# Batch 0's input products in float32 from decoded, unsplit weights, and a float64 decoding by one multiplication and two merging passes, in a fused attention and gated feed-forward kernel

## The chip, the cores and the metric

One core of a Trainium2 chip runs the whole program in one launch. The metric is the device time of one execution in microseconds. Lower is better.

## The reference, cut to what matters

The inputs are q, k and v, each (8 batches, 8 heads, 576 positions, 64) in float32, and the weights of a gated feed-forward layer. Attention is the sum of a local banded one (distance under 4) and one over positions averaged by fours. Its output, (8, 576, 512), is the `x` of the second function.

```python
def _attn_ref(q, k, v):
    ...
    out_d = sm_attn(q_d, k_d, v_d)
    out_up = np.repeat(out_d, factor, axis=2)
    ...
    out_local = np.matmul(attn, v)
    return (out_up + out_local).astype(np.float32)

def _moe_ref(x, w_in, w_spatial, b_spatial, w_out):
    h = np.maximum(x @ w_in, 0.0)
    u, v = (h[..., :d_ff // 2], h[..., d_ff // 2:])
    mu = np.mean(v, axis=-1, keepdims=True)
    var = np.mean((v - mu) ** 2, axis=-1, keepdims=True)
    v_n = (v - mu) / np.sqrt(var + 1e-06)
    v_s = np.einsum('ts,bsd->btd', w_spatial, v_n) + b_spatial[None, :, None]
    gated = u * v_s
    return (gated @ w_out).astype(np.float32)
```

`w_in` (512 x 1024) and `w_out` (512 x 512) arrive as float64 and are passed on as their bit patterns; `w_spatial` (576 x 576) is float32. The chip decodes the float64 itself.

## The kernel before, in words

**Units of work.** Eight heads are four pairs, two heads on 128 partitions. `attention(n)` (L610) handles one pair of one batch, 32 in all; `gated(b)` (L827) handles one batch's feed-forward layer. The engines are PE (matmul), DVE (VectorE), ACT (ScalarE), POOL (GpSimd) and SP (which issues most DMAs).

**A pair.** SP loads q and k (L624). POOL or DVE sums groups of four positions in two steps (`sum1`, `sum2`, L631 and L634). PE computes the local scores in 64 x 64 blocks of float32 (L663), with the mask added either by two matmuls of PE (L656) or by DVE (L676). DVE takes maximum, difference, sum and inverse (L685 to L698), ACT the exponential (L704), DVE or POOL the norm (L708). PE transposes the probabilities (L716), ACT copies them out (L718), PE multiplies by the values (L796). The pooled part runs beside it: scores (L728, float32, three matmuls of 144 columns), exponential (L737), norm (L749 or L751), transposes (L764), values (L782) against `tv`, the pooled v. `tv` is one plain DMA (L579) and three accumulating DMAs, which POOL issues one after the other (L581). DVE adds both parts into `xf` (L806, L808). Then x is split: ACT writes the high half, scaled to float16 (L814), DVE the low half, the difference (L816), and ACT packs the last 64 positions (L818). The scale is that of the batch: ACT sums the absolute values of v (`vabs`, L598), and `bound` (L394) makes a power of two of them by a transpose, a maximum, a spreading matmul and five short DVE instructions (L404 to L415).

**Weights.** `piece64` (L442) decodes 128 rows of 512 float64: WV and WU are the two halves of `w_in` (four pieces each), WO is `w_out` (four). DVE masks out the exponent bits (`e1`, L453), ACT rescales them (`e2`, L458), DVE puts the sign in (`e3`, L463), makes the mantissa from the high word (`m1`, L468), adds the low one (`m2`, L472), and DVE or POOL multiplies both (`m3`, L476 or L478). The result, `mb`, has five buffers. WSP is `w_spatial`, five pieces (`piece32`, `piece_tail`). WV, WU and WSP then get a common scale each (`wabs`, L558, and `bound`) and are split into a high and a low float16 half (`split`, L426 on ACT, L429 on DVE). Every product uses three of the four combinations of halves (`PAIRS`).

**A batch's feed-forward layer.** V pieces (L844): for each of four tiles of 128 positions, 3 x 4 matmuls of 512 columns; for the last 64 positions, 8 matmuls with both halves of x packed on 128 partitions (L849). Each is evicted by ACT, normalised by DVE and POOL, and split again. U pieces (L899): four feature tiles, each in two stretches of 256 and 320 positions, 12 matmuls. S pieces (L917 to L920) multiply by `w_spatial`, DVE multiplies by U, and the result is split into float32r halves; O pieces (L955) multiply by WO.

**The order.** Nothing is issued as the loops stand in the code. Every operation is handed to a `Plan` with an engine, a duration, its buffers and a rank, and `Plan.run` (L132) lays out one order for every engine: on each it takes the lowest rank among the operations that could begin within `NEAR` ns of the first. Ranks are an offset by the kind of operation (`RANK`, `MRANK`, `WRANK`) plus the pair's number. `ON` holds a letter per pair or piece, which says where an operation that has several ways runs (P for POOL, D for DVE, A for ACT, T for a mask by PE); the last letter counts for all that follow. Each engine executes its own list in order. Where the plan expects PE to idle in the first 110 us, it puts in dummy matmuls (`warm`, L992), which compute nothing. Buffers of a tag are handed out in the order in which they were asked for; the staging tiles of `piece64` (`stg`, four) thus go to WV, WU and WO in turn.

Of the kernel before, what the change touches and what calls it, by code (L numbers as in the profile page):

```python
# [76 lines left out]
class Plan:  # L77
# [19 lines left out]
    def op(self, eng, ns, fn, r=(), w=(), hold=(), after=(), rank=0.0, lag=None, port=False, kb=0, mode="",  # L97
# [8 lines left out]
        o.eng, o.ns, o.fn, o.rank, o.lag, o.port, o.kb, o.name = eng, ns, fn, rank, lag, port, kb, name  # L106
# [25 lines left out]
    def run(self, near=150.0, stay=0.0, dma=(1500.0, 4.2, 500.0), emit=True):  # L132
# [16 lines left out]
        while left:  # L149
# [60 lines left out]
            stop = t + o.ns  # L210
# [44 lines left out]
MRANK = {"V": [[-2.464, 0.981], [12.511, 0.226], [-2.435, 0.048]],
        "U0": [[8.716, 6.0], [3.119, 6.0], [7.419, 0.756]],
        "S0": [[-31.809, 0.01], [1.553, 0.075], [8.037, 1.094]],
        "U1": [[30.903, 2.091], [4.504, 0.01], [5.941, 0.268]],
        "O0": [[23.009, 0.398], [16.009, 0.093], [8.369, 0.044]],
        "S1": [[4.955, 0.875], [37.534, 0.04], [5.267, 0.763]],  # L260
        "O1": [[26.479, 0.073], [0.158, 0.01], [-14.194, 0.078]]}
EVICT = 8.0
WRANK = {"WV": [-3.775, 1.863],
        "WU": [-0.347, 0.057],
        "WSP": [3.494, 0.477],
        "WO": [5.623, 0.082]}
# [771 lines left out]
```

## Time and profile before

| What | Value |
|---|---|
| Median of 3 runs | 603.85 us (603.24 to 605.93) |
| Span of the profiled execution, first to last instruction | 603.0 us |
| PE busy | 572.9 us, 95% |
| DVE busy | 421.2 us, 70% |
| ACT busy | 352.8 us, 59% |
| POOL busy | 155.0 us, 26% |
| Moved by DMA | 56.95 MB |

The profiled execution has no time of its own beside its span; the timed runs include what lies around the span. Busy shares are means over stages with different limits, so the windows by stage are to be read beside them. Dummy matmuls count as busy. Matmuls overlap in the pipeline: a mean duration per matmul is longer than the distance of two of them, and the distance is what a piece of work costs.

### The profile page before, as it was taken

The page shows a single profiled execution, that of the slowest core. Times are in us where ns is not written, and L with a number is a line of the kernel's source. Part 1 is how long each engine was busy: PE and PEld are TensorE (multiplying, and loading weights), DVE is VectorE, ACT ScalarE, POOL GpSimd, SP SyncE. Part 2 cuts the span into 40 slices and gives each one's busy share as a digit, 9 for nine tenths or more (in the row PEclk, how much of TensorE's full clock was granted, in tenths as well). Part 3 has the DMA queues.
Part 4 walks back from the last instruction along what each step waited for, and adds up shares of the span by engine and source line. Part 5 has one row for each costly group of instructions (what it writes and reads, how often), then busy time and mean ns, then how long its engine had stood idle before and what let it go on. Part 6 is the DMA issues. An engine that isn't in the chain of part 4 may idle for free.

```text
span 603.0 us, 14807 instructions
## 1 busy us (share of the span) xinstructions
PE 572.9 (95%) x6004; PEld 421.6 (70%) x6004; DVE 421.2 (70%) x1013; ACT 352.8 (59%) x911; POOL 155.0 (26%) x165
## 2 busy tenths in 40 slices
PE   5488799999999999999999999999999999999996
PEld 2264657777688766777687858787687867775774
DVE  5499989998896865856788837875688677336230
ACT  3499779757766655665566636664566555334331
POOL 4214534204531140412322122213322122102100
PEclk9567789999999999999999999999999999999999
DMA  8886631624331641405241342305231200000002
GB/s 269 226 274 204 152 105 50 133 63 137 83 115 41 195 82 37 123 2 138 57 141 63 97 98 98 123 8 140 66 124 41 76 19 37 0 37 0 36 1 87
DMA packets 37263, 56.95 MB, mean 94 GB/s; under 512 B 3530, under 2 KB 24010, under 8 KB 37196
## 3 DMA queue, kind: packets, MB, share of 16 engines
q1 hardware_dynamic: 34892, 48.94, 25.4%
q0 software_dynamic: 2304, 7.08, 7.3%
q8 instruction: 47, 0.77, 0.5%
q14 instruction: 20, 0.16, 0.1%
HBM read 46.57 MB, written 9.44 MB: 93 GB/s over the span
## 4 chain that ended last, share of the span: by engine, by line
PE 85%; DMA 6%; ACT 4%; DVE 2%; issue 1%; POOL 1%; SPq 1%; ACTq 0%; POOLq 0%
PE pmb L917 5%; PE pma L844 5%; PE pmb L955 5%; PE pma L899 4%; PE pma L955 4%; DMA tva<-v_dram 4%; PE pmd L844 4%; PE pmc L917 4%; PE pmd L899 4%; PE pmd L955 4%; PE pmc L955 4%; PE pmb L899 4%; PE pmc L844 3%; PE pmc L899 3%; PE pma L917 3%; PE pab L796 2%
## 5 line engine op out<-in xcount | busy, mean ns | idle before, releaser
L899 PEld LDWEIGHTS <-win 128*128 128x128 f16 x768 | 74.4, 98 | 18.9 <-issue 0.9
L917 PEld LDWEIGHTS <-vha 128*128 128x128 f16 x768 | 73.4, 98 | 19.3 <-issue 0.8
L917 PE MATMUL pmb<-wsp,vha 128*128 128x320 f16 (+1 forms) x276 | 37.8, 286 | 0.0
L751 POOL TENSOR_TENSOR eda<-eda,smda 96x432 f32<-96x432 f32 x13 | 12.8, 984 | 76.7 <-ACT ua L902 37.9
L708 POOL TENSOR_TENSOR sa<-sa,sma 128x640 f32<-128x640 f32 x12 | 16.2, 1350 | 55.4 <-ACT gta L927 23.9
L917 PE MATMUL pmc<-wsp,vha 128*128 128x256 f16 (+1 forms) x216 | 28.8, 283 | 0.0
L708 POOL TENSOR_TENSOR sb<-sb,smb 128x640 f32<-128x640 f32 x14 | 19.6, 1401 | 35.6 <-PE pab L663 10.6
L872 POOL TENSOR_TENSOR stc<-stc,mhalf 128x1 f32<-128x1 f32 (+1 forms) x13 | 10.9, 838 | 53.3 <-DVE stc L856 53.3
L751 POOL TENSOR_TENSOR edb<-edb,smdb 96x432 f32<-96x432 f32 x13 | 14.4, 1105 | 39.8 <-DVE smdb L742 38.6
L917 PE MATMUL pma<-wsp,vha 128*128 128x320 f16 (+1 forms) x168 | 23.6, 290 | 0.0
L992 PE MATMUL pma<-mask_b,mask_a 128*128 128x512 bf16 x53 | 19.1, 495 | 3.2 <-DVE sw L506 3.2
L955 PE MATMUL pma<-wo,gb 128*128 128x512 f32 x84 | 21.3, 402 | 0.0
L581 POOL DMA_DIRECT2D tva<-v_dram x12 | 11.1, 927 | 31.3 <-DMA tva<-v_dram 31.2
L872 POOL TENSOR_TENSOR sta<-sta,mhalf 128x1 f32<-128x1 f32 (+1 forms) x14 | 11.4, 813 | 29.0 <-DVE sta L856 28.9
L955 PEld LDWEIGHTS pma<-wo,gb 128*128 128x128 f32 x84 | 15.6, 188 | 3.7
L955 PE MATMUL pmb<-wo,ga 128*128 128x512 f32 x72 | 18.1, 400 | 0.0
L844 PEld LDWEIGHTS <-xa 128*128 128x128 f16 x96 | 9.4, 99 | 10.9 <-issue 0.2
L638 ACT ACTIVATE qda<-kda 64x144 f32<-64x144 f32 x32 | 10.3, 321 | 11.2 <-POOL kda L634 7.4
L704 ACT ACTIVATE sb<-sb 128x640 f32<-128x640 f32 x16 | 11.8, 738 | 8.3 <-DVE sb L682 7.6
L872 POOL TENSOR_TENSOR stb<-stb,mhalf 128x1 f32<-128x1 f32 (+1 forms) x13 | 10.4, 800 | 21.4 <-DVE stb L856 21.4
L694 DVE TENSOR_REDUCE smb<-sb 128x10 f32<-128x640 f32 x16 | 12.9, 806 | 4.3 <-ACT sb L704 4.3
L955 PEld LDWEIGHTS pmb<-wo,ga 128*128 128x128 f32 x72 | 13.4, 188 | 3.2
(740 smaller groups left out, 1688.9 us busy)
## 6 DMA issues: line engine op xcount, KB each, us to landing
qka<-qk_dram SPq DMA_DIRECT2D x16, 576.0 KB, 3.7
qkb<-qk_dram SPq DMA_DIRECT2D x16, 576.0 KB, 13.6
tva<-v_dram POOLq DMA_DIRECT2D x12, 288.0 KB, 4.8
tvb<-v_dram POOLq DMA_DIRECT2D x12, 288.0 KB, 4.4
stg<-w_in_dram SPq DMA_DIRECT2D x4, 512.0 KB, 4.6
more<-w_in_dram SPq DMA_DIRECT2D x4, 512.0 KB
out_dram<-rowc SPq DMA_DIRECT2D x8, 256.0 KB, 2.1
out_dram<-rowb SPq DMA_DIRECT2D x8, 256.0 KB, 2.0
```

The costliest lines, as they stand in the source:

```text
L581: plan.op("POOL", 850, lambda r=r: nc.gpsimd.dma_start(t.ap, v4[b, r], accum_op=ALU.add), w=[t], rank=rank + 2.0 + 0.3 * r, kb=288, name="tv")
L694: nc.vector.tensor_reduce(sm.ap, s.ap, axis=AX.X, op=ALU.add)
L704: exp_of.append(plan.op("ACT", 643, lambda: nc.scalar.activation(s.ap, s.ap, AF.Exp, scale=1.0 / 8.0), w=[s], rank=R["E"], name="exp"))
L708: plan.op(nm, 0, lambda: side(nm).tensor_tensor(s.ap, s.ap, sm.ap[:, :, None].broadcast_to([P, NW, 64]), op=ALU.mult), r=[sm], w=[s], rank ...
L751: side(nd).tensor_tensor(ed.ap, ed.ap, smd.ap[:96, :, None].broadcast_to([96, 3, G]), op=ALU.mult)
L796: nc.tensor.matmul(pv.ap[h * 64:h * 64 + 64, c:c + QB[w + 1] - QB[w]], vb.ap[k, w], pT.ap[k, blk, q0:q0 + QB[w + 1] - QB[w]], start=True, ...
L844: nc.tensor.matmul(ps.ap, xs[c].ap[:, i, t * P:(t + 1) * P], win[:, c, j, FF:], start=(c == 0 and (i, j) == (0, 0)), stop=(c == NC - 1 and ...
L872: plan.op("POOL", 530, lambda: nc.gpsimd.tensor_tensor(st.ap[:r, 8:9], st.ap[:r, 8:9], mhalf[:r], op=ALU.pow), w=[st], rank=rank - EVICT, ...
L899: nc.tensor.matmul(ps.ap[:, :n], win[:, c, i, ft * P:(ft + 1) * P], xs[c].ap[:, j, HA[h]:HA[h + 1]], start=(c == 0 and (i, j) == (0, 0)), ...
L917: nc.tensor.matmul(ps.ap[:, :n], vh.ap[:, c, i, fs], wsp[:, c, j, hs], start=(c == 0 and (i, j) == (0, 0)), stop=False)
L955: nc.tensor.matmul(ps.ap, g.ap[:, c, i, k:k + P] if t < NT else gt.ap[:, c, i], wo[:, c, j, :], start=(c == 0 and (i, j) == (0, 0)), stop= ...
L992: nc.tensor.matmul(ap.rearrange("p (j k) -> p j k", k=64), mask_a, mask_b[:, None, :].broadcast_to([P, 8, 64]), start=True, stop=True)
```

## The change

It does these things:
- `piece64` decodes by four operations where it had six: `low` shifts the low word right by 29 (DVE), `shrink` multiplies the high word, read as a float32, by 2^-112 (ACT or DVE by a letter of `ON`), `body` shifts that left by three and merges the low bits (DVE), `sign` merges the sign (DVE). POOL has no part in it.
- With `FULL = 1`, batch 0 is `whole`: its x is kept in float32 in the place of its two float16 halves. `vabs`, the batch's scale, `xhi`, `xlo` and `xtail` are gone for it. Its V pieces are 4 float32 matmuls of 512 columns (five pieces, the last one not packed), its U pieces 4 float32 matmuls; both read the decoded weights `plain`, ahead of scale and split. WV and WU are still scaled and split for the batches that follow.
- The mask by PE is four matmuls on quarters of the array where it was two on the whole array; the letters of `mask` change.
- Staging tiles: three for four. `mb`: eight for five. The bias row is loaded into a tile of `xf`.
- The planner: durations are set anew, PE's work counts 1.5 times before 70 us, an accumulating DMA lands later the more is in flight, and all ranks and letters are new, so that the order of every engine differs over the whole span.

The diff, cut to its core:

```diff
+            ns = o.ns * SLOW[1] if o.mode and t < SLOW[0] else o.ns
+            stop = t + ns
...
+                more = min(4000.0, 0.5 * max(0.0, moved - t))
                 moved = max(moved, t + dma[0]) + o.kb * dma[1]
-                stop = t + dma[0] + 2 * o.kb * dma[1] + 2 * dma[2] if o.eng == "POOL" else moved + dma[2]
+                stop = t + dma[0] + 2 * o.kb * dma[1] + 2 * dma[2] + more if o.eng == "POOL" else moved + dma[2]
...
-RANK = {"load": [-0.34, 10.998, -8.45],
+RANK = {"load": [-44.57, 114.48, 16.68],
+        "vload": [85.3, -193.17, -137.58],
+        "vabs": [-38.15, -134.56, -81.97],
+        "tv": [-162.84, -70.55, 81.87],
...
-NEAR = 101.242
-STAY = 9.309
+WRANK = {"WV": [73.85, 2.37],
+        "WU": [-22.18, 0.03],
+        "WSP": [47.61, 0.01],
+        "WO": [-1.45, 9.22]}
+NEAR = 94
+STAY = 95.4
 WARM = 110000.0
-ON = {"sum": "PDPPPPDPD",
-        "m3": "PDDPPPDPDDPD",
-        "mask": "TTTTTDTTD",
-        "norm": "DDDDDPDPP",
-        "normd": "PADAAPAAP",
-        "vlo": "DPDPPPPDPPD"}
+SLOW = (70000.0, 1.5)
+FULL = 1
+MB = 8
+ON = {"shrink": "DDADAAADDA",
+      "sum": "PPDPPDDPDDDPDPDPDPPDPDPDDDPDDDPD",
+      "mask": "DDTTTDTTDTDDDDDDTDDDDDDTDDTD",
+      "norm": "DPPPDDPDPDDPPPPPPPDPDPPPDDPDPPDP",
+      "normd": "DDAAPDPDADAPDDPPPPADPPADPDDPAAD",
+      "vlo": "PDPPDPPPPDDDPDDDPPDDDPDDDDPDDDPPDPDPPPD"}
...
-    more = const.tile([P, 2, 2 * FF], F32, name="more")
-    plan.tag("stg", [stg[:, 0], stg[:, 1], more[:, 0], more[:, 1]])
+    more = const.tile([P, 2 * FF], F32, name="more")
+    plan.tag("stg", [stg[:, 0], stg[:, 1], more])
...
-    places("mb", 5, [P, FF], F32)
+    places("mb", MB, [P, FF], F32)
     places("wst", NT + 1, [P, S], F32)
-    places("bias", 1, [P, S], F32)
...
-        def e1():
+        def low():
             lo, hi = words()
-            nc.vector.tensor_scalar(eb.ap.bitcast(I32), hi, 0x7FF00000, None, op0=ALU.bitwise_and)
-        def e2():
-            e = eb.ap.bitcast(I32)
-            nc.scalar.activation(e, e, AF.Relu, bias=rebias, scale=8.0)
-        def e3():
+            nc.vector.tensor_scalar(mb.ap.bitcast(I32), lo, 29, None, op0=ALU.logical_shift_right)
+        def shrink():
             lo, hi = words()
-            e = eb.ap.bitcast(I32)
-            nc.vector.scalar_tensor_tensor(e, hi, -2**31, e, op0=ALU.bitwise_and, op1=ALU.bitwise_or)
-        def m1():
-            lo, hi = words()
-            nc.vector.tensor_scalar(mb.ap.bitcast(I32), hi, 0x000FFFFF, 0x00100000, op0=ALU.bitwise_and, op1=ALU.bitwise_or)
-        def m2():
-            lo, hi = words()
-            nc.vector.scalar_tensor_tensor(mb.ap, lo.bitcast(U32), 2.0**-32, mb.ap.bitcast(I32), op0=ALU.mult, op1=ALU.add)
-        def m3():
-            if pr.eng == "POOL":
-                nc.gpsimd.tensor_tensor(mb.ap, mb.ap, eb.ap, op=ALU.mult)
+            if sh.eng == "ACT":
+                nc.scalar.activation(eb.ap, hi.bitcast(F32), AF.Copy, scale=2.0**-112)
             else:
-                nc.vector.tensor_tensor(mb.ap, mb.ap, eb.ap, op=ALU.mult)
-        plan.op("DVE", 335, e1, r=[t], w=[eb], hold=[mb], rank=rank, port=True, name="e1")
-        plan.op("ACT", 618, e2, w=[eb], rank=rank, name="e2")
-        plan.op("DVE", 335, m1, r=[t], w=[mb], rank=rank, port=True, name="m1")
-        plan.op("DVE", 602, m2, r=[t], w=[mb], rank=rank, port=True, name="m2")
-        plan.op("DVE", 602, e3, r=[t], w=[eb], rank=rank, port=True, name="e3")
-        pr = Way("m3", {"WV": 0, "WU": NC, "WO": 2 * NC}[key[0]] + key[1], P=("POOL", 1251, True), D=("DVE", 602, True))
-        plan.op(pr, 0, m3, r=[eb], w=[mb], rank=rank, name="m3")
-        done = lambda: split(dst_hi, dst_lo, lambda: mb.ap, 2.0**-20, [mb], rank, FF, key)
+                nc.vector.tensor_scalar(eb.ap, hi.bitcast(F32), 2.0**-112, None, op0=ALU.mult)
+        def body():
+            m = mb.ap.bitcast(I32)
+            nc.vector.scalar_tensor_tensor(m, eb.ap.bitcast(I32), 3, m, op0=ALU.logical_shift_left, op1=ALU.bitwise_or)
+        def sign():
+            m = mb.ap.bitcast(I32)
+            nc.vector.scalar_tensor_tensor(m, eb.ap.bitcast(I32), -2**31, m, op0=ALU.bitwise_and, op1=ALU.bitwise_or)
+        sh = Way("shrink", {"WV": 0, "WU": NC, "WO": 2 * NC}[key[0]] + key[1], A=("ACT", 618, False), D=("DVE", 335, True))
+        plan.op(sh, 0, shrink, r=[t], w=[eb], hold=[mb], rank=rank, name="shrink")
+        plan.op("DVE", 335, low, r=[t], w=[mb], rank=rank, port=True, name="low")
+        plan.op("DVE", 602, body, r=[eb], w=[mb], rank=rank, port=True, name="body")
+        plan.op("DVE", 602, sign, r=[eb], w=[mb], rank=rank, port=True, name="sign")
+        done = lambda: split(dst_hi, dst_lo, lambda: mb.ap, 1.0, [mb], rank, FF, key)
+        if FULL and key[0] != "WO":
+            plain[key[0]].append(mb)
...
-        tb = fetch([(bsp.broadcast_to([2, S]), TAIL)], rank, 8, "bias")
+        tb = fetch([(bsp.broadcast_to([2, S]), TAIL)], rank, 8, "xf")
...
-                    nc.tensor.matmul(t[:, h, :NBLK], mask_a, mask_b[:, None, :].broadcast_to([P, NBLK, 64]),
-                                     start=True, stop=False)
+                    for i in range(2):
+                        m = slice(i * 64, i * 64 + 64)
+                        r = slice(h * 64, h * 64 + 64)
+                        nc.tensor.matmul(t[m, h, :NBLK], mask_a[r, r], mask_b[r, None, :].broadcast_to([64, NBLK, 64]),
+                                         start=True, stop=False)
...
+        xf = x if whole else plan.buf("xf")
         x_of.setdefault(b, []).append(x)
-        xt = tail_of[b]
+        def plane():
+            return x.ap.rearrange("p i t -> p (i t)").bitcast(F32) if whole else xf.ap
...
+        plan.op("DVE", 795, both, r=[pv, dn], w=[x.sub(0) if whole else xf], rank=R["AV"] - EVICT, name="xf")
+        if whole:
+            return
+        sx, xt = sx_of[b][0], tail_of[b]
...
+                if whole:
+                    for c, x in enumerate(planes()):
+                        nc.tensor.matmul(ps.ap[:r], x[:, t * P:t * P + r], plain["WV"][c].ap, start=(c == 0), stop=(c == NC - 1))
+                elif t < NT:
...
+            if whole:
+                plan.op("PE", NC * 854, mm, r=xr + plain["WV"], w=[ps], hold=[vr, vh if t < NT else vt], rank=rank, lag=PEL + 60, mode="F", name="V")
+                plan.op("ACT", 586, lambda: nc.scalar.activation(vr.ap[:r], ps.ap[:r], AF.Relu), r=[ps], w=[vr], rank=rank - EVICT, name="relu")
...
+                if whole:
+                    for c, x in enumerate(planes()):
+                        nc.tensor.matmul(ps.ap[:, :n], plain["WU"][c].ap[:, ft * P:(ft + 1) * P], x[:, HA[h]:HA[h + 1]],
+                                         start=(c == 0), stop=(c == NC - 1))
+                    return
```

## Rows read from the trace of the kernel before

**Rows 1.** The page: busy time and share, and the granted clock in 40 slices.

```profile
PE 572.9 (95%) x6004; PEld 421.6 (70%) x6004; DVE 421.2 (70%) x1013; ACT 352.8 (59%) x911; POOL 155.0 (26%) x165
...
PEclk9567789999999999999999999999999999999999
```

**Rows 2.** Windows, whole kernel: stretch, length, busy us per engine (instructions), clock, DMA, GB/s.

```profile
0.00:78.58 78.58, 54.57 (x588) 35.52 (x589) 59.30 (x138) 55.34 (x140) 27.37 (x40) 0.72 0.78 228
78.58:200.00 121.42, 121.35 (x1422) 90.34 (x1421) 109.43 (x263) 86.24 (x235) 39.53 (x40) 1.00 0.34 88
200.00:590.00 390.00, 389.19 (x3964) 289.87 (x3964) 252.43 (x613) 209.45 (x535) 88.07 (x86) 1.00 0.25 70
590.00:603.00 13.00, 7.75 (x34) 5.90 (x32) 0.00 (x0) 1.76 (x3) 0.00 (x0) 0.93 0.24 81
```

**Rows 3.** Windows of line 992 alone, before the first product (PE, PEld, clock, DMA).

```profile
0.00:78.58 78.58, 19.12 (x53) 5.83 (x53) 0.72 0.78 228
```

**Rows 4.** Chain of waits, full-clock pieces on PE: start us, us, line, instructions.

```profile
84.97 2.59 PE pma L844 x12
...
90.89 1.73 PE pmc L849 x8
...
94.68 0.25 PE pmb L764 x3
...
95.18 1.31 PE pmc L899 x12
96.49 0.73 PE pmd L728 x6
97.22 0.55 PE pab L716 x5
97.77 0.65 PE pmb L782 x8
98.42 0.38 PE paa L656 x2
98.80 0.74 PE paa L663 x40
99.54 0.68 PE pab L796 x40
...
116.07 1.63 PE pmc L899 x12
```

**Rows 5.** Chain at the beginning, and DVE's longest wait (us in total, times, longest).

```profile
14.31 7.26 DMA tva<-v_dram
...
DVE mxda L732 <- PE pmb L728: 8.1, 1, 8.1
```

**Rows 6.** Timeline of DVE before the first product: start us, us, line, out<-in.

```profile
12.44 0.68 DVE L478 TENSOR_TENSOR mbb<-mbb,rowb 128x512 f32<-128x512 f32 x1
...
14.58 0.41 DVE L453 TENSOR_SCALAR rowd<-more 128x512 int32<-128x512 int32 x1
...
31.78 0.15 DVE L412 TENSOR_SCALAR sw<-sw 128x1 int32<-128x1 int32 x1
...
38.38 0.75 DVE L429 SCALAR_TENSOR_TENSOR win<-mbd,sw,win 128x512 f16<-128x512 f32 x1
...
48.98 0.82 DVE L816 SCALAR_TENSOR_TENSOR xa<-xfa,sxa,xa 128x576 f16<-128x576 f32 x1
...
68.97 2.51 DVE L816 SCALAR_TENSOR_TENSOR xc<-xfa,sxa,xc 128x576 f16<-128x576 f32 x1
...
74.42 0.26 DVE L808 TENSOR_TENSOR xfb<-pab,dnb 128x112 f32<-128x112 f32 x1
```

**Rows 7.** SP queue's wait for a staging tile; timeline of GpSimd, two instructions.

```profile
SPq L438 <- DVE rowa L463: 6.7, 1, 6.7
...
24.57 1.27 POOL L476 TENSOR_TENSOR mbd<-mbd,rowd 128x512 f32<-128x512 f32 x1
...
69.42 1.43 POOL L631 TENSOR_TENSOR suma<-qka 128x576 f32<-128x576 f32 x1
```

More of the change, by code (lines that the diff above doesn't have):

```diff
@@ L417, in bound @@
         plan.op("DVE", 190, greatest, r=[pb], w=[tok], rank=rank - EVICT, name="great")
[L418 to L419 removed]
+        plan.op("PE", 300, spread, r=[tok], w=[pb], rank=rank, lag=PEL, mode="F", name="spread")
+        plan.op("DVE", 695, scales, r=[pb], w=[tok], rank=rank - EVICT, port=True, name="scale")
     def split(dst_hi, dst_lo, src, scale, toks, rank, n, key):
@@ L438, in go @@
                 nc.sync.dma_start(t.ap.bitcast(src.dtype)[lo:lo + src.shape[0], :src.shape[1]], src)
-        plan.op("SP", 60 * len(parts), go, w=[t], rank=rank - 4.0, kb=kb, name="fetch")
+        plan.op("SP", 450 * len(parts), go, w=[t], rank=rank - 4.0, kb=kb, name="fetch")
         return t
@@ L510, in piece_tail @@
         plan.op("DVE", 60, zero, w=[("zero",)], rank=rank, name="zero")
-        plan.op("ACT", 580, ab, r=[tb, ("zero",)], w=[("sum", "WSP", k)], rank=rank, name="wabs")
+        plan.op("ACT", 700, ab, r=[tb, ("zero",)], w=[("sum", "WSP", k)], rank=rank, name="wabs")
     def tail_done(t, tb, rank, rows):
@@ L562, in tile_kernel @@
             toks.append(("sum", k, NT + 1))
-        bound(lambda i=i: sw[:, i], len(toks), toks, ("sw", i), rank, 0.0, -10.0 if k == "WSP" else -20.0, 50.0)
+        bound(lambda i=i: sw[:, i], len(toks), toks, ("sw", i), rank, 0.0, -10.0 if k == "WSP" else 0.0, 50.0)
         for done, t, rank, n in later[k]:
@@ L612, in attention @@
         R = {k: n + v[min(n // NP, 2)] for k, v in RANK.items()}
+        whole = b < FULL
         if p == 0:
             load_down(b)
-            tail_of[b] = plan.buf("xtail")
+            if not whole:
+                tail_of[b] = plan.buf("xtail")
         tv = tv_of[b]
@@ L643, in attention @@
         for h in range(2):
-            plan.op("ACT", 215, lambda h=h: sum3(h), r=[kb], w=[qb.sub(h)], rank=R["sum"], name="sum3")
+            plan.op("ACT", 165, lambda h=h: sum3(h), r=[kb], w=[qb.sub(h)], rank=R["sum"], name="sum3")
         ps, s, mx, sm = plan.buf("pa"), plan.buf("s"), plan.buf("mx"), plan.buf("sm")
-        sc = Way("mask", n, T=("PE", 1100, False), D=("PE", 640, False))
+        sc = Way("mask", n, T=("PE", 780, False), D=("PE", 640, False))
         pe_mask = sc.pick == "T"
@@ L827, in gated @@
     def gated(b):
-        xs, xt = x_of[b], tail_of[b]
+        whole = b < FULL
+        xs, xt = x_of[b], tail_of.get(b)
         xr = [x.sub(i) for x in xs for i in range(2)]
         vh, vt = plan.buf("vh"), plan.buf("vt")
-        iv = sx_of[b][1]
+        iv = None if whole else sx_of[b][1]
+        planes = lambda: [x.ap.rearrange("p i t -> p (i t)").bitcast(F32) for x in xs]
         vtok = []
```

133 lines of the change are left out of this document (63 added, 70 removed).

## Prediction, made before the changed kernel was run

> **What bounds the kernel now.** I read the page first. PE is busy 95% of the span, so the first look says that TensorE is the bound and that more work on it must cost [rows 1]. The windows by stage say where that is true. From 78.58 to 590 us PE stands still for 0.07 + 0.81 us in all; that is the steady state. Ahead of it, in the first 78.58 us, PE is busy 54.57 us [rows 2], and 19.12 us of this are the dummy matmuls of L992, which compute nothing [rows 3]. The granted clock there is 0.72 on average, with slices at 0.5 to 0.7; behind 78.58 us it is 1.00 [rows 1, 2]. At 78.58 us the first input product of batch 0 starts; I call that moment the start. What ends the span is thus the start, plus all PE work that is left by then, plus the 5.25 us of the drain (13.00 less 7.75 in the last stage) [rows 2].
>
> How much useful work is done before the start? I price it by pieces at full clock [rows 4]: scores 0.74 us (and 0.38 for the mask matmuls, where PE adds the mask), pooled scores 0.73, two transposes of pooled probabilities 2 x 0.25, their values 0.65, the transposes 0.55, the values 0.68. That is 3.85 us for an attention pair without a mask. By the order of the code and the matmul counts, 6 scores (5 with a mask), 6 pooled scores and 4 of each other kind lie before the start: 6 x 0.74 + 5 x 0.38 + 6 x 0.73 + 4 x (0.50 + 0.65 + 0.55 + 0.68) = 20.2 us. So 78.6 - 20.2 = 58.4 us of the span are lost by PE at the beginning, and that is what a change can win back.
>
> What holds the start? VectorE (DVE) is busy 59.30 of these 78.58 us, ScalarE 55.34 [rows 2]. In the chain of waits the beginning belongs to the accumulating DMAs of tv, the last of 7.26 us, for which GpSimd's queue stands ahead of its first pooling sum; for this DVE waits 8.1 us in one piece [rows 5]. Then the chain runs through ACT and DVE to xf of the fourth pair, which DVE finishes at 74.42 + 0.26 = 74.7 us [rows 6]; scaling, splitting and the first product follow.
>
> **The products (PE, on the path).** Removed are 12 half-precision matmuls a piece: V takes 2.59 us a tile (four tiles) and 1.73 for the tail, U 1.31 and 1.63 (four each) [rows 4]: 10.4 + 1.7 + 5.2 + 6.5 = 23.8 us. Added are four float32 matmuls a piece. The pooled scores are float32 matmuls in this trace: three of 144 columns, six records, in 0.73 us [rows 4], or 1.69 ns a column. V has 4 x 512 columns a piece, 3.46 us, five pieces as the tail is no longer packed: 17.3. U has 4 x 256 and 4 x 320: 1.73 and 2.16 us, four each: 15.6. Together 32.9: **9.1 us more** on PE, which nothing hides, as PE is full behind the start. The mask matmuls become four quarters of the array where they were two whole ones: 7 pieces at 0.38 go, 9 come. Between quarters that all run side by side (9 x 0.19 = 1.7 us) and quarters in turn (9 x 0.76 = 6.8) the change is -1.0 to +4.2; twenty small float32 scores take 0.74 us, so quarters do overlap [rows 4], and I take 0.
>
> **The start (DVE's ledger).** I count what no longer stands on DVE ahead of xf of the fourth pair.
> - Decoding: eight pieces (WV, WU) lie before it. One took two single-input instructions of 0.41 us (L453, L468) and two of 0.68 (L463, L472, as long as L478), and three of the eight a product on DVE, 0.68 (L478) [rows 6]: 8 x 2.18 + 3 x 0.68 = 19.5. Now: one at 0.41, two at 0.68, and on four pieces the shrinking multiplication, 0.41: 8 x 1.77 + 4 x 0.41 = 15.8. It saves 3.7.
> - The low parts of x (L816) of three pairs: 0.82, another that I count as 0.82, and 2.51 [rows 6]: 4.2, gone for batch 0.
> - Splitting WV and WSP, nine instructions of 0.75 [rows 6], 6.8: not gone, but the float32 products don't wait for WV's, so these can stand behind.
> - Four scale computations of six short instructions, about 0.15 each [rows 6]: 3.6, one gone and three that can stand behind.
>
> Together 18.3 us. Batch 1's first scores also lie ahead of xf; I leave them there against WU's decoding, which V doesn't need. With 0.3 us for the semaphore, the start is 74.7 - 18.3 + 0.3 = 56.7 us; the scaling to float16 behind xf is gone too. Its ends: no advance beyond the removed tail, 74.7; and 8.1 us more, 48.6, if the new order also takes away DVE's long wait for tv [rows 5]. The order is computed anew with a landing time for accumulating DMAs that grows with the transfers ahead of them, which is what held this wait, so I take off half of the 8.1: **the start comes at 53 us**.
>
> The **other engines**: ACT loses the exponent step of the pieces that shrink on DVE, four absolute sums, four high parts and four tail copies of batch 0. It is at 55.34 of 78.58 [rows 2], behind DVE, so I take nothing for it. On SP the staging tiles go from four to three. The nearest row is a fetch that already waited 6.7 us for DVE to free one [rows 7], and the loads of later pairs stand behind it in SP's queue. The freed decoding time shortens the hold, so I take 0, between -6.7 and +6.7. The bias row goes through a tile of xf that is unused then, at nothing; if it were in use, it would delay only WSP's bound, which batch 0's products don't read. The eight tiles of decoded weights (five before) hold WV and WU until both the split and batch 0's products have read them, so WO's decoding waits for V; the products' 33 us cover its four pieces (4 x 1.77 on DVE), and without that cover batch 0's first output piece would come some 7 us later. The GpSimd products of decoding go: of the eight pieces five were there, 1.27 us each or 6.3 in all [rows 7]. The rows differ on what that gives DVE: L816 took 2.51 instead of 0.82 while GpSimd summed for 1.43 us [rows 6, 7], but GpSimd will carry sums again in the new order. I take 0.
>
> The Trainium skill ("SBUF — State Buffer", section "SBUF: two separate sides") states that GpSimd and a VectorE operation with two SBUF inputs exclude each other for the whole instruction. By that rule the five products gone would give all their time to DVE, and the sum would end 6.3 us earlier, at 586.5. The trace agrees for L816, and the rule speaks equally against the change's new sums on GpSimd, since the new `body` and `sign` have two SBUF inputs.
>
> **The sum.** At 53 us four pairs are done, two of them with a mask: 4 x 3.85 + 2 x 0.38 = 16.2 us. The loss is 53 - 16.2 = 36.8 instead of 58.4: 21.6 won. Paid are 9.1 for float32 and the clock: products now run in slices that had 0.7 [rows 1], at worst 20 us at 0.77 or 4.6 us, at best nothing, since a dense stream had 1.00 [rows 2]; I take 1.5. All ranks change, so the order after the start does too. A better one can win 0.9 us of stalls; a worse drain could double the 5.25 [rows 2]; I take 0. Net: 21.6 - 9.1 - 1.5 = **11.0 us less**, 592.0 against the span of 603.0. The median of the runs, 603.85, lies 0.85 above the span, so the forecast is 592.85, said as **593**; the rivals' times are counted from 603.85 too.
>
> **The rivals.**
> 1. *Start earlier still.* The tv wait goes whole, and half of the five GpSimd products' 6.3 us with it; the start comes at 56.7 - 8.1 - 3.2 = 45.4: loss 29.2, net 29.2 - 10.6 = 18.6 less, 585 us. For: DVE idles 8.1 us in one piece. Against: DVE is also busy 109.43 of 121.42 us behind the start [rows 2] and must follow.
> 2. *DVE becomes the bound behind the start.* Splits and scales that I moved back come to lie between 60 and 110 us, where PE wants batch 1's operands. Of DVE's 18.3 us only 8.8 are gone (3.7 + 4.2 + 0.9), and 8.8 us is then all that the start can be worth: 8.8 - 10.6 is 1.8 us slower, 605.7. For: 90% busy there. Against: the float32 products are 33 us during which PE asks for nothing new.
> 3. *Slower: the pairs, not the decoding, hold the start.* The third and fourth pair pass two score buffers and two q/k tiles; if that chain keeps its time, xf of the fourth pair stays at 74.7 and only the scaling behind it goes. The loss is 74.7 - 20.2 = 54.5, won 3.9 - 10.6: 6.7 us slower, 610.5. It decides as soon as the start lies later than 64 (16.2 + 58.4 - 10.6). For: the long ACT and DVE chain through the pairs. Against: DVE's order is rewritten as well.
> 4. *The products are no true float32.* If they ran in one pass, PE would do less work than before, some 15 us less, and the time would be below 580. Against: the tiles are declared float32, as those of the pooled scores.
>
> **How the numbers follow.** Forecast 0.48, rival 1 0.18, rival 2 0.17, rival 3 0.15, rival 4 0.02. The forecast's own ends are 588 (a start at 48.6: 58.4 - 32.4 - 10.6 = 15.4 less) and 602. A measurement of this kernel can tell about 0.5%, 3 us, from no change. Faster by more than that: 0.43 of the forecast, rivals 1 and 4: 0.63. Within: 0.05 of the forecast and 0.12 of rival 2: 0.17. Slower: 0.05 of rival 2 and rival 3: 0.20. The range takes in the forecast, rival 2 and about half of rivals 1 and 3: 583 to 610.
>
> **What would show it.** Right: the first product (V) at about 53 us; about 3.46 us a V piece and 1.73 or 2.16 a U piece; fewer dummies than 53; PE without stalls behind; the clock at 1.00 within some us of the start. Wrong: a V start beyond 64 us (rival 3), PE idle of several us between 60 and 130 us waiting for DVE (rival 2), or a start below 48 (rival 1).

## The result, and the profile after

The changed kernel takes **589.78 us** (median) against 603.79 us of the kernel before, measured beside it: a ratio of 0.975, 95% interval 0.972 to 0.978, or 14 us less. One of its four timed runs took 932.38 us at a granted clock of 0.61 and is left out of the ratio; the other three lie between 589.29 and 589.90. The forecast was 593 us with a range of 583 to 610. The span of the profiled execution is 588.1 us, 14.9 less than before.

The page of the changed kernel, busy time and share, and the clock in 40 slices, to be read against [rows 1]:

```profile
PE 564.7 (96%) x5948; PEld 416.0 (71%) x5948; DVE 394.7 (67%) x974; ACT 344.2 (59%) x898; POOL 147.2 (25%) x166
...
PEclk9878899999999999999999999999999999999999
```

PE is still the engine that is nearly always busy. Less of the beginning ran at a lowered clock: its first seven slices read 9878899, in tenths of full speed, where 9567789 stood.

Windows of the changed kernel by stage, with the columns of [rows 2]. The first product now starts at 50.84 us instead of 78.58; the line behind the windows is that product in PE's timeline:

```profile
0.00:50.84 50.84, 34.35 (x509) 23.32 (x509) 38.22 (x90) 34.75 (x96) 19.11 (x33) 0.89 0.92 265
50.84:78.00 27.16, 25.49 (x124) 12.38 (x127) 23.99 (x67) 18.94 (x53) 9.33 (x10) 0.90 0.44 128
78.00:200.00 122.00, 121.92 (x1448) 95.19 (x1444) 98.84 (x240) 81.96 (x221) 33.92 (x35) 1.00 0.44 117
200.00:575.00 375.00, 375.00 (x3850) 279.05 (x3848) 233.61 (x580) 206.62 (x528) 84.87 (x89) 1.00 0.24 66
575.00:588.10 13.10, 7.90 (x34) 6.01 (x32) 0.00 (x0) 1.88 (x4) 0.00 (x0) 0.89 0.25 80
```

```profile
50.84 1.92 PE L850 MATMUL pmb<-mba,xa 128*128 128x512 f32 x2
```

Up to the start DVE is busy 38.22 us where it was 59.30, and idle 12.6 us where it was 19.3. Of the 27.7 us by which the start came forward, 21.1 are thus less work on DVE ahead of it and 6.7 less waiting. The window behind the start holds something new: PE idles 27.16 - 25.49 = 1.67 us there, at a clock of 0.90. From 78 us on PE stands still for 0.08 us; in the kernel before it was 0.88 from its start on.

What the products cost is read from the chain of waits of the changed kernel (start us, us, line, instructions):

```profile
61.69 5.40 PE pmd L850 x8
67.08 3.43 PE pma L850 x8
...
95.33 2.15 PE pmc L912 x8
97.48 1.73 PE pmb L912 x8
...
110.44 0.26 PE pab L655 x4
110.70 0.58 PE pab L662 x40
```

A V piece takes 3.43 us at full clock, a U piece 1.73 or 2.15. The third V piece, at 61.69 us, took 5.40: it stood behind the stall, and the clock fell. The stall itself, among PE's waits:

```profile
PE pmd L850 <- ACT rowb L872: 1.7, 1, 1.7
```

The last two rows of the chain are a score with a mask: 0.26 + 0.58 us where it was 0.38 + 0.74 [rows 4].

Two timelines show how the beginning was rearranged. GpSimd's:

```profile
4.67 1.03 POOL L572 DMA_DIRECT2D tva<-v_dram  x1 [0.72 <-DMA tva<-v_dram]
5.86 1.14 POOL L627 TENSOR_TENSOR suma<-qka 128x576 f32<-128x576 f32 x1 [0.16 <-DMA qka<-qk_dram]
...
13.09 0.84 POOL L572 DMA_DIRECT2D tva<-v_dram  x1 [3.38 <-DMA tva<-v_dram]
...
20.80 0.83 POOL L572 DMA_DIRECT2D tva<-v_dram  x1 [1.25 <-DMA tva<-v_dram]
```

The first pooling sum (L627) stands between the first and the second accumulating DMA of tv (L572) and begins at 5.86 us. In the kernel before it stood behind the third one, which GpSimd could issue only at 21.86 us, when the second had landed at the end of the 7.26 us [rows 5]. The two rows of the kernel before:

```profile
21.86 0.83 POOL L581 DMA_DIRECT2D tva<-v_dram  x1 [6.70 <-DMA tva<-v_dram]
22.41 1.46 POOL L631 TENSOR_TENSOR suma<-qka 128x576 f32<-128x576 f32 x1
```

DVE's timeline in the changed kernel:

```profile
8.56 0.89 DVE L675 TENSOR_TENSOR sa<-paa,mask 128x384 f32<-128x384 f32 x2 [5.42 <-PE paa L662]
...
22.95 0.81 DVE L430 SCALAR_TENSOR_TENSOR wsp<-wsta,sw,wsp 128x576 f16<-128x576 f32 x1
...
26.59 0.68 DVE L465 SCALAR_TENSOR_TENSOR mba<-rowa,mba 128x512 int32<-128x512 int32 x1
...
49.32 0.26 DVE L810 TENSOR_TENSOR xd<-pab,dnb 128x112 f32<-128x112 f32 x1
```

xf of the fourth pair is done at 49.32 + 0.26 = 49.6 us, before it was 74.7 [rows 6]. DVE's wait of 8.1 us for the first pooled scores is gone whole; its longest wait ahead of the start is now the one of 5.42 us for the first local scores. The decoding's merging step takes 0.68 us, as the old one did. The split of WSP (L430) still stands **ahead** of the start, at 22.95 us.

### The profile page after: what moved, and what is told of

It is laid out like the page before. It is cut to its first block, busy times and chain, and to the rows that moved or that the text cites. A ratio compares the mean times of both kernels' runs of the same rounds, so it can differ in the third digit from the quotient of the medians.

```text
span 588.1 us, 14642 instructions
## 1 busy us (share of the span) xinstructions
PE 564.7 (96%) x5948; PEld 416.0 (71%) x5948; DVE 394.7 (67%) x974; ACT 344.2 (59%) x898; POOL 147.2 (25%) x166
## 4 chain that ended last, share of the span: by engine, by line
PE 90%; DVE 4%; ACT 3%; issue 1%; DMA 1%; POOL 0%; POOLq 0%; ACTq 0%; DVEq 0%
PE pmb L976 6%; PE pmb L938 5%; PE pmd L917 4%; PE pmd L854 4%; PE pmd L976 4%; PE pma L938 4%; PE pmc L976 4%; PE pmd L938 4%; PE pmc L938 4%; PE pmb L917 3%; PE pma L976 3%; PE pma L854 3%; PE pma L917 3%; PE pmc L917 3%; PE pmc L854 3%; PE pmb L854 2%
## 5 line engine op out<-in xcount | busy, mean ns | idle before, releaser
L917 PEld LDWEIGHTS <-win 128*128 128x128 f16 x672 | 64.9, 98 | 17.2 <-issue 0.8
L938 PE MATMUL pmd<-wsp,vha 128*128 128x256 f16 (+1 forms) x180 | 23.7, 281 | 0.0
L938 PE MATMUL pmc<-wsp,vha 128*128 128x256 f16 (+1 forms) x168 | 22.9, 286 | 0.0
L707 POOL TENSOR_TENSOR sb<-sb,smb 128x640 f32<-128x640 f32 x11 | 14.2, 1295 | 26.1 <-DVE smb L697 14.1
L627 POOL TENSOR_TENSOR suma<-qka 128x576 f32<-128x576 f32 x7 | 8.2, 1172 | 35.7 <-DVE ud L956 17.1
L572 POOL DMA_DIRECT2D tva<-v_dram x12 | 10.5, 878 | 23.4 <-DMA tva<-v_dram 23.4
L703 ACT ACTIVATE sa<-sa 128x640 f32<-128x640 f32 x16 | 11.8, 738 | 7.5 <-DVE sa L681 5.1
L627 POOL TENSOR_TENSOR suma<-qkb 128x576 f32<-128x576 f32 x7 | 9.0, 1291 | 26.2 <-DMA qkb<-qk_dram 10.1
L976 PEld LDWEIGHTS pmb<-wo,ga 128*128 128x128 f32 x72 | 13.4, 188 | 3.1
L572 POOL DMA_DIRECT2D tvb<-v_dram x12 | 10.2, 854 | 19.3 <-DMA tvb<-v_dram 19.3
L976 PE MATMUL pmb<-wo,gb 128*128 128x512 f32 x60 | 15.1, 400 | 0.0
L634 ACT ACTIVATE qdb<-kdb 64x144 f32<-64x144 f32 x32 | 10.2, 320 | 6.5 <-POOL kdb L630 4.8
```

Of the source, the lines that this page charges most:

```text
L572: plan.op("POOL", 850, lambda r=r: nc.gpsimd.dma_start(t.ap, v4[b, r], accum_op=ALU.add), w=[t], rank=rank + 2.0 + 0.3 * r, kb=288, name="tv")
L627: side(s1).tensor_tensor(sb.ap.rearrange("p x (g r) -> p x g r", r=2), x[:, :, :, :2], x[:, :, :, 2:], op=ALU.add)
L634: nc.scalar.mul(qb.ap[r, :, h], kb.ap[r, 0].rearrange("p (a q) -> p a q", a=3), 1.0 / 128.0)
L703: exp_of.append(plan.op("ACT", 643, lambda: nc.scalar.activation(s.ap, s.ap, AF.Exp, scale=1.0 / 8.0), w=[s], rank=R["E"], name="exp"))
L707: plan.op(nm, 0, lambda: side(nm).tensor_tensor(s.ap, s.ap, sm.ap[:, :, None].broadcast_to([P, NW, 64]), op=ALU.mult), r=[sm], w=[s], rank ...
L917: nc.tensor.matmul(ps.ap[:, :n], win[:, c, i, ft * P:(ft + 1) * P], xs[c].ap[:, j, HA[h]:HA[h + 1]], start=(c == 0 and (i, j) == (0, 0)), ...
```

## The experiments

Twelve kernels were run. Each gives a ratio to the kernel before, measured beside it; the median of that one moved between 603.8 and 605.1 us, so the ratios are what is compared, with that of the changed kernel, 0.975. A thousandth is 0.6 us. The changed kernel's own interval is 1.6 us to either side, and it enters every difference.

### Parts undone with the order computed again

Three runs undo parts of the change and let the planner lay out the order with the new ranks.

```diff
# full0
-FULL = 1
+FULL = 0
# olddec: the six operations of the decoding before; 2^-20 goes into two evictions of batch 0
-ON = {"shrink": "DDADAAADDA",
+ON = {"m3": "PDDPPPDPDDPD",
# order_only: both
...
```

> The changed kernel with FULL = 0: all batches use split float16 halves, while the decoding, the ranks, the letters and the quarter masks stay new. My theory (the start sets the time, and float32 lets it come early): the start moves back from 50.8 us by the split of WV (four low halves, 3.0 us on VectorE), four low parts of x (3.3) and two scales (2), so to 57 to 62 us, and PE is rid of 8.9 us; 588 to 594 us. Rival A (the new order of loads alone brings the start, float32 is only a cost): the start stays near 51 us and the time falls to about 581. Rival B (float32 is worth far more, because it takes the whole preparation of batch 0 away): the start goes back beyond 65 us, 598 or more.

> The changed kernel with the old six-operation decoding (three of the eight products of WV and WU on VectorE, five on GpSimd), batch 0 still in float32; the factor 2^-20 of the old decoding is taken back in the two evictions of batch 0. My theory: VectorE works 3.7 us longer ahead of the start and the exponent step goes through ScalarE again, so the start comes 3 to 6 us later and the time is 592 to 596. Rival A (the decoding is hidden beside the loads of the pairs): the start moves by less than 1 us and the time is 589 to 591. Rival B (the products on GpSimd block VectorE for their whole length): the start comes 8 us later or more, 598 and above.

> The changed kernel with FULL = 0 and the old decoding: against the kernel before only the ranks, the letters, the planner's durations, the buffers and the quarter masks are new. My theory: about the sum of the two effects above, start at 62 to 68 us, 594 to 600 us, so that the new order alone is worth 4 to 10 us. Rival A (the order is everything): 585 or less. Rival B (the order is worth nothing without the two other parts): 601 or more.

Measured: 629.7 us (ratio 1.043, 1.039 to 1.048), 619.3 (1.025, 1.021 to 1.029) and 633.7 (1.049, 1.045 to 1.053). All three are slower than the kernel before, by more than any theory had put on a part. The times lie in the open ends of the last rivals (598 or more, 598 and above, 601 or more), but the windows give another reason than theirs, the run with the new order alone first, then the changed kernel over the same 150 us:

```profile
0.00:150.00 150.00, 106.06 (x1224) 69.64 (x1225) 126.94 (x299) 99.13 (x257) 51.31 (x64) 0.83 0.61 166
```

```profile
0.00:150.00 150.00, 131.84 (x1422) 90.12 (x1423) 125.36 (x304) 103.62 (x273) 48.99 (x63) 0.94 0.62 172
```

In the first one PE was idle for 44 of these 150 us; its first input product, a U piece in these three runs, started at 104.7 us (84.7 with the old decoding and 89.2 with FULL = 0). The ranks are numbers fitted to one list of operations. Another list under the same ranks gives a quite different order, and such a run measures that order. It shows only that the new ranks carry no gain of their own; what float32 or the decoding is worth can't be read from it. So all later runs **keep the order of every engine as it is** and change one thing in it: the planner decides as before, its list of issues is kept, and one entry is moved, lengthened or left out.

### Is PE the bound behind the start?

```diff
-for c, x in enumerate(planes()):
+for c, x in enumerate(planes()[:2]):
...
-start=(c == 0), stop=(c == NC - 1))
+start=(c == 0), stop=(c == 1))
```

> The changed kernel, but the U pieces of batch 0 sum over two of the four pairs of heads: half of their products are left out, 7.8 us of PE work. My theory (PE is the bound from the start on): the time falls by 7 to 8 us, to about 582. Rival (VectorE is the bound behind the start, so PE work in this stretch is partly hidden): it falls by less than 4 us, and PE shows new idle time between 80 and 130 us.

Measured: 587.9 us, ratio 0.9729 (0.969 to 0.977); the half that is left out takes 4 x 0.86 + 4 x 1.08 = 7.8 us off PE, but the time falls by about 1.3 us, within the intervals. The windows from 78 to 120 us, of this run and of the changed kernel, then PE's waits of this run and the first row of its third V piece:

```profile
78.00:120.00 42.00, 38.86 (x503) 30.32 (x504) 40.59 (x88) 29.12 (x74) 9.30 (x10) 0.96 0.48 129
```

```profile
78.00:120.00 42.00, 42.00 (x489) 33.80 (x485) 39.02 (x85) 28.45 (x70) 8.48 (x9) 1.00 0.46 122
```

```profile
PE pmc L912 <- ACT ub L923: 2.3, 1, 2.3
PE pmc L912 <- ACT ue L923: 0.8, 1, 0.8
```

```profile
61.81 2.08 PE L850 MATMUL pmd<-mba,xa 128*128 128x512 f32 x2 [2.99 <-ACT rowb L872]
```

With less to do PE idles 3.14 us for ACT's evictions of U and gets a clock of 0.96, while DVE is busy 40.59 of 42 us. DVE and ACT set the pace there as much as PE does. A part of the missing gain lies elsewhere: the third V piece, the same work in both kernels, took 6.74 us instead of 5.40 at the lower clock, and the fourth one started 1.5 us later than in the changed kernel. The spans, 587.1 and 588.1 us, differ by 1.0; without those 1.5 us some 2.5 of the 7.8 would be left, by my estimate, still within the rival's 4 us. My theory, that PE alone is the bound from the start on, falls.

### What of DVE's work is on the path?

Three runs change DVE's work at the head, each with the order kept:

```diff
# low_twice: twice in every weight piece
+for _ in range(2):
     nc.vector.tensor_scalar(mb.ap.bitcast(I32), lo, 29, None, op0=ALU.logical_shift_right)
# low_none: the shift left out, the merge without it
-nc.vector.scalar_tensor_tensor(m, eb.ap.bitcast(I32), 3, m, op0=ALU.logical_shift_left, op1=ALU.bitwise_or)
+nc.vector.tensor_scalar(m, eb.ap.bitcast(I32), 3, None, op0=ALU.logical_shift_left)
# xlo_back: behind each xf of batch 0, into a tile of its own
+nc.vector.scalar_tensor_tensor(spare, plane(), 2.0, plane(), op0=ALU.mult, op1=ALU.subtract)
```

> The changed kernel with every engine's order as it is, but the right shift of the decoding runs twice on VectorE in each of the twelve weight pieces (the second one writes the same words). That puts 0.34 us on VectorE for each, 2.7 us for the eight pieces of WV and WU and 4.1 in all, close to what the shorter decoding saved there (3.7 by my count). Theory now (VectorE is nearly full from 8 to 130 us, before the start and behind it): the time rises by 2.5 to 4.5 us, to 592 to 594. Rival (the decoding is hidden beside the pairs and the products): less than 1 us.

> The changed kernel, order as it is, but the right shift of the low words is left out and the merging shift has one input: the weights lose their last three mantissa bits. VectorE works 12 x (0.34 + 0.27) = 7.3 us less, 4.9 of it for WV and WU. Theory (VectorE's work ahead of the start is on the path): the reverse of the run with the shift twice, 2.5 to 4.5 us less, 585 to 587. Rival (the loads of the weights, which come behind those of q, k and WSP, hold the start now, so less work on VectorE turns into waiting): less than 1 us, and VectorE or ScalarE waits for a transfer ahead of 50 us.

> The changed kernel, order as it is, with one VectorE instruction more behind each of the four pairs of batch 0: as long as the low half of x was in the kernel before (0.75 us or more), writing a tile that nothing reads. Theory (float32 helps by what it takes off VectorE ahead of the start): the start comes 2.5 to 3.5 us later and the time rises by 2 to 4 us, to 592 to 594. Rival (ScalarE or the chain of the pairs holds the start): less than 1 us.

Measured: 594.1 us with the shift twice (ratio 0.9805, 0.975 to 0.986), 587.7 without it (0.9706, 0.969 to 0.973), 592.7 with the dummy low halves (0.9796, 0.978 to 0.981). Against 0.975 these are +3.3, -2.7 and +2.8 us, for +4.1, -7.3 and +3.2 us of work (the four dummy operations took 0.76, 0.90, 0.76 and 0.76 us). With the intervals of both ratios the three are uncertain by about 3.6, 2.0 and 1.8 us. The first is thus not clear of the noise by its ratio alone, but its trace bears it out: the third V piece starts at 64.86 us instead of 61.69. So DVE's work is on the path, and not only ahead of the start: with the shift twice the first product came at 51.94 us, 1.1 later, and with the dummy low halves at 52.46, 1.6 later, less than the 2.5 to 3.5 expected; the rest was lost behind it. PE's wait for the eviction of the second V tile, with the shift twice, and with the dummy low halves:

```profile
PE pmd L851 <- ACT rowb L873: 3.9, 1, 3.9
```

```profile
PE pmd L853 <- ACT rowb L875: 3.0, 1, 3.0
```

It was 1.7 us in the changed kernel. The run without the shift gave back less than half of what it took off; 2.7 us lies at the theory's lower end. Its first product came at 49.61 us, and what holds DVE in it is no transfer, as the rival had it, but ACT's copy of the pooled values of the fourth pair, a wait of 1.1 us in the changed kernel:

```profile
DVE xd L808 <- ACT dnb L787: 1.9, 1, 1.9
```

### What of the order is on the path?

```diff
# wsp_ahead: SP's queue
-tv0, q/k of pair 0, q/k of pair 1, WSP loads and bias, ...
+tv0, WSP loads and bias, q/k of pair 0, q/k of pair 1, ...
# tv_ahead: GpSimd's queue
-tv, sum1, sum2, sum1, sum2, tv, norm, tv, ...
+tv, tv, tv, sum1, sum2, sum1, sum2, norm, ...
# before_moved: the kernel before, both the other way round
+q/k of pairs 0 and 1, tv0, weights, ...       tv, sum1, sum2 (pair 0), ..., tv, ...
```

> The changed kernel with one move on SP's queue: the seven loads of WSP and the bias, 1.4 MB, stand ahead of the first two loads of q and k, as most of them did in the kernel before; the order of every other engine is unchanged. Theory (q and k first is a part of the early start): at about 280 GB/s the first scores come some 5 us later, the start too, and the time rises by 3 to 5 us, to 593 to 595. Rival (what arrives early waits for VectorE anyway): less than 1 us.

> The changed kernel with one move on GpSimd: the three accumulating DMAs of tv stand ahead of the first pooling sum, as they did in the kernel before; nothing else moves. Theory (the wait for tv that held VectorE for 8.1 us in the kernel before is gone by this order): the first pooled scores come after the third tv DMA was issued, at 15 to 21 us instead of 9.5; VectorE waits in order, the start comes 6 to 11 us later and the time is 596 to 601. Rival (the wait costs nothing, since VectorE's early idle time is covered by the loads): below 591.

> The kernel before with two moves in its own order: the first two loads of q and k to the head of SP's queue, and on GpSimd both pooling sums of the first pair ahead of the second and third accumulating DMA of tv. Float16 halves, six-operation decoding and all else stay. Theory (the order at the head is worth this much by itself, since VectorE's wait of 8.1 us for the first pooled scores goes): the first product starts 5 to 9 us earlier than 78.6 and the time falls by 5 to 9 us, to 595 to 599. Rival (without float32 the scaling and splitting hold the start, or the loads of weights that now land later do): less than 2 us.

Measured: loads of WSP ahead 596.0 us (ratio 0.9838, 0.979 to 0.989), start at 56.10, 5.3 us later, as the theory had it; PE waited for q and k:

```profile
PE paa L681 <- DMA qka<-qk_dram: 5.8, 1, 5.8
```

The tv DMAs ahead of the sums: **604.2 us** (0.9986, 0.996 to 1.001). This one move gives the whole gain of the change away. The start came at 65.24 us, 14.4 later; the theory had 6 to 11. GpSimd's timeline of that run, and DVE's longest wait:

```profile
20.19 0.82 POOL L591 DMA_DIRECT2D tva<-v_dram  x1 [6.29 <-DMA tva<-v_dram]
21.07 1.14 POOL L646 TENSOR_TENSOR suma<-qka 128x576 f32<-128x576 f32 x1
```

```profile
DVE mxda L750 <- PE pmb L746: 13.6, 1, 13.6
```

The first sum starts at 21.07 us instead of 5.86, and DVE, which executes in order, waits 13.6 us for the pooled scores behind it. It is the same wait that took 8.1 us in the kernel before [rows 5], only longer. The traces fit an explanation that was not tried by itself: in the kernel before the weights are loaded first and DVE decodes them up to 17.3 us, while here q and k come first, the first scores are early, and no decoding stands ahead of the wait in DVE's list.

The other way round, in the kernel before: 601.3 us (0.9934, 0.992 to 0.995), 4.0 us faster, start at 75.05. DVE's waits there:

```profile
DVE rowa L474 <- DMA stg<-w_in_dram: 5.4, 1, 5.4
...
DVE mxda L753 <- PE pmb L749: 0.8, 1, 0.8
```

The wait for the pooled scores fell from 8.1 us to 0.8, but now DVE waits 5.4 us for the first weights, which land later, where it was 2.7. A part of what was won went there, and the start came 3.5 us earlier, at 75.05. That is less than the theory's 5 to 9 us and more than the rival's 2. So these two moves, with float16 halves and the old decoding, are worth 4 us and not the 14 that the reverse move of GpSimd's sums costs.

### Is the new stall worth anything?

```diff
# relu_first: ACT's queue behind the first V eviction
-relu (tile 0), ..., wabs, vhi (tile 0), relu (tile 1), ...
+relu (tile 0), ..., vhi (tile 0), relu (tile 1), wabs, ...
# relu_early
-relu (tile 0), ..., wabs, vhi (tile 0), relu (tile 1), ...
+relu (tile 0), ..., relu (tile 1), vhi (tile 0), wabs, ...
```

> The changed kernel with one move on ScalarE: the eviction of the second V tile stands ahead of the absolute sum of the sixth weight piece, for which ScalarE waits 1.6 us while PE waits for the eviction. Theory (the stall of 1.7 us on PE at 60 us and the half clock behind it, 2.0 us in the third V piece, are on the path): the time falls by 2 to 4 us, to 586 to 588. Rival (VectorE is the bound there, PE would stall later instead): less than 1 us.

> The changed kernel, order as it is but for ScalarE: the eviction of the second V tile stands ahead of the absolute sum of a weight piece and of the float16 copy of the first V tile, for which ScalarE waits for VectorE. The run before this moved it ahead of the sum alone, and the stall of PE stayed. Theory (the stall of 1.7 to 2.8 us on PE at 60 us and the half clock behind it are on the path): the stall goes and the time falls by 2 to 4 us, to 586 to 588. Rival (PE comes to wait for VectorE later by as much, since VectorE is full): less than 1 us.

Measured: 590.0 us (ratio 0.9735, 0.969 to 0.978) and 590.7 us (0.9766, 0.975 to 0.978): no difference that the intervals allow to be told, in either direction. In the first one the eviction still stood behind the float16 copy of the first tile, which waits for DVE, so the stall stayed; in the second it was gone, and PE waited for the eviction of a later V tile instead. PE's waits, first run and second:

```profile
PE pmd L870 <- ACT rowb L892: 2.8, 1, 2.8
```

```profile
PE pma L749 <- ACT rowd L894: 3.3, 1, 3.3
```

So the rivals hold. The traces say the same: in the run of the first move the first pair of matmuls of the first V piece took 1.02 us, at the full clock, where the changed kernel's took 1.92; the stall was longer by 1.1 us, and the third V piece started at 61.80 us, against 61.69. PE only had to wait longer. The stall is a symptom. V's evictions, statistics and weight decoding pass through ACT and DVE together, and PE meets their pace at one tile or the next.

## Why the prediction was right, point by point

**The price of the products** held: 5 x 3.43 + 4 x (1.73 + 2.15) = 32.7 us, 8.9 more than before (forecast 9.1). That a price from three matmuls of 144 columns carries over to 512 columns is thereby shown, and rival 4, products in one pass, is out.

**The start** came at 50.84 us, forecast 53, ends 48.6 and 74.7. The total was nearly right, and that is in part luck, because its terms were not. Up to xf of the fourth pair DVE is busy 36.95 of 49.58 us, where it was 56.53 of 74.68: 19.6 us less work (18.3 in the ledger) and 5.5 less waiting (4 in the ledger). But decoding takes 10.0 us there instead of 21.0, 11.0 less where the ledger had 3.7: WU's four pieces went behind the start, which I had set off against batch 1's scores. Against that, only WV's low halves, 3.0 us, went behind it, where the ledger had 6.8 for WV and WSP; WSP's stayed ahead, 3.8 us. The wait for tv, of which I had taken half, went whole, but 5.42 us of waiting for the first scores came in its place. That DVE's work ahead of the start is on the path was shown by lengthening the decoding and by putting the low halves of x back. That the wait for tv was a matter of GpSimd's queue was the best guess in the ledger, and the move that brings it back shows it: the start came 14.4 us later. Rival 1 had the wait right, but a start at 45.4 did not come.

**GpSimd's products and the lock.** The prediction set the gain from their going at 0. By the rule that it cites from the Trainium skill ("SBUF — State Buffer", section "SBUF: two separate sides"), that GpSimd and a VectorE operation with two SBUF inputs exclude each other for the whole instruction, its estimate was 6.3 us, with the end at 586.5. Where the two engines meet, the row agrees with the rule. GpSimd and DVE in the changed kernel, at the third weight piece:

```profile
42.54 1.14 POOL L627 TENSOR_TENSOR suma<-qka 128x576 f32<-128x576 f32 x1
43.76 1.00 POOL L630 TENSOR_TENSOR kda<-suma 128x288 f32<-128x288 f32 x1
```

```profile
42.72 1.51 DVE L469 SCALAR_TENSOR_TENSOR mbc<-rowc,mbc 128x512 int32<-128x512 int32 x1
44.15 0.88 DVE L461 TENSOR_SCALAR rowd<-stg 128x512 f32<-128x512 f32 x1
```

The second merging step (L469), two inputs, takes 1.51 us beside GpSimd's sum where it otherwise takes 0.68, and the shrinking multiplication 0.88 beside the next sum, where it otherwise takes 0.42; that one has a single input, so it is not a case of the rule as cited. But these are sums that now lie where the products lay, as the prediction had said against the rule; with 0.85 instead of 0.42 for one shift (31.86 us) DVE loses 0.83 + 0.46 + 0.43 = 1.7 us ahead of the start. What it had lost to the products before is in the other trace. DVE's two rows there that were longer than usual beside a product, and the products:

```profile
9.47 1.50 DVE L468 TENSOR_SCALAR mbb<-stg 128x512 int32<-128x512 int32 x1
52.40 0.96 DVE L478 TENSOR_TENSOR mbb<-mbb,rowb 128x512 f32<-128x512 f32 x1
```

```profile
9.30 1.39 POOL L476 TENSOR_TENSOR mba<-mba,rowa 128x512 f32<-128x512 f32 x1 [3.37 <-DVE rowa L463]
51.08 1.73 POOL L476 TENSOR_TENSOR mba<-mba,rowa 128x512 f32<-128x512 f32 x1 [5.31 <-DVE rowa L463]
```

They usually take 0.42 and 0.68, so the five products lengthened DVE's work by at most 1.08 + 0.28 = 1.4 us and not 6.3. The forecast's 0 is close, since 1.4 us went and 1.7 came.

**The clock and the stall** were under-sized: 1.5 us in the forecast; measured are 1.7 us of stall, 4.42 - 3.43 = 1.0 us for the first V piece (50.84 to 55.26 us) and 5.40 - 3.43 = 2.0 for the third, 4.7 together. This is what PE lost; as the second move on ACT shows, taking the stall away gave nothing back, so it is not a price of its own.

**The masks**, taken at 0 between -1.0 and +4.2, gave 7 x 1.12 + 25 x 0.64 - 9 x 0.84 - 23 x 0.64 = 1.6 us of PE work back over the whole span, as the scores behind them run faster too (an unmasked score piece takes 0.64 us in both traces).

**The sum with what was measured**, at the prices of the forecast: before the new start lie 5 scores (3 with a mask), 5 pooled scores and 4 of each other kind, 18.0 us; the loss is 50.84 - 18.0 = 32.8 instead of 58.4, so 25.6 us won. Less 8.9 and 4.7, plus 0.6 for the masks and 0.8 for stalls that went behind the start: 13.4 of the 14.9 us between the spans. Of the masks' 1.6 us only some 0.6 count here, because the scores ahead of either start are already in the 20.2 and the 18.0. Where the other 1.5 us come from is open. The forecast of 11.0 missed by the start (4.0 us), the masks and the stalls on one side and by the clock on the other.

**Rival 2**, DVE as the bound behind the start, lost as a forecast of the time but is partly true: PE work taken out at 80 to 105 us is worth little, about 1.3 of 7.8 us, and DVE work added there or ahead costs most of its length, 3.3 of 4.1 and 2.8 of 3.2 us. I had weighed it against PE's 33 us of products, as if these were time during which DVE catches up; DVE was busy 23.99 of 27.16 us there and did not. **Rival 3**, a start that stays with the pairs, did not come: DVE took up the first pair's scores at 8.56 us, where it was 17.36.

What stays open is how much of the 14 us float32 brings as such. The run without it had ranks that were not made for it, and a kernel with float16 halves and an order fitted as carefully was not tried. What float32 takes off DVE for x, put back, cost 2.8 us; the split of WV and the scales, which it allows to come later, were not put back alone.

The run without the shift took 587.7 us, the least of all with the half U; it leaves out the last three bits of each decoded weight's mantissa, so it is not a better form of the same computation. Of the runs that keep all of it none is faster than the changed kernel beyond the intervals.

## What to carry to other kernels

When engines work through fixed lists in order, find the first instruction in each list that waits for a slow transfer: moving a few short operations past it can be worth as much as a rewritten computation. Here 14 us hung on four pooling sums of 0.7 to 1.2 us each, in the changed kernel's order; a like move in the old order, together with one of loads, gave 4. Experiments on such a kernel must keep the lists fixed, because with a planner that is given another list of operations one measures its luck with that list. And an engine that is 100% busy behind the start isn't proof that its work is the bound: take some of it away and see.

## What was not expected of the hardware

An accumulating DMA of 288 KB from GpSimd's queue, with the loads of q, k and weights in flight, held the next one for 6 to 7 us (issues at 13.06 and 20.19 us in the run with the tv DMAs ahead), against a median of 4.6 us from issue to landing that the page of the changed kernel has for both groups of twelve.

And the stall of PE of 1.67 us was followed, not accompanied, by a lower clock in the trace of the changed kernel. Windows of the changed kernel, with the columns of [rows 2]:

```profile
58.00:63.00 5.00, 3.33 (x14) 1.93 (x13) 4.79 (x12) 2.76 (x7) 2.50 (x3) 1.00 0.79 238
63.00:64.00 1.00, 1.00 (x3) 0.40 (x2) 0.90 (x7) 0.69 (x4) 0.40 (x1) 0.53 0.01 4
64.00:65.00 1.00, 1.00 (x3) 0.48 (x2) 0.96 (x5) 1.00 (x6) 0.00 (x0) 0.50 0.00 0
...
66.00:67.00 1.00, 1.00 (x3) 0.27 (x2) 1.00 (x3) 0.00 (x0) 0.00 (x0) 0.76 0.63 111
67.00:78.00 11.00, 11.00 (x91) 5.68 (x93) 8.52 (x27) 8.38 (x22) 4.35 (x5) 1.00 0.16 53
```

The stall ends at 61.69 us and the clock is still 1.00 up to 63; then it is at half, 1.2 GHz of 2.4, for 3 us, and back at 1.00 from 67 on. The second to fourth matmul pairs of the third V piece took 1.44 to 1.91 us there, where the same pair takes 1.02 with its overlap. In the run with half of U, the stall of 2.99 us ended at 61.81 us, and the clock had already fallen within it (0.78 from 60 to 62 us, 0.50 from 62 on).
